# A new instruction plan for a fused recurrence and gated unit: transfers in plan order, three x buffers, gates multiplied in place

## The chip, the cores and the metric

One core of one Trainium2 chip runs the kernel. The time is the device time of the core in microseconds; the median of eight runs is compared. Five engines run side by side, each through its own list of instructions, in order: PE (matrix products and transposes), DVE (vector), ACT (activation functions), POOL (GpSimd) and SP (here it only issues loads). Results of PE stand in PSUM, eight banks of 512 fp32 columns; everything else stands in SBUF.

## What is computed

Inputs are x and two gates of 4 x 6336 x 256, a vector of 256 and three small weights. The first half is a gated linear recurrence over time, the second a gated unit with a causal convolution of five taps:

```python
a_t = np.exp(c * sig_r * np.log(np.clip(a_base, 1e-06, 1.0 - 1e-06))[None, None, :])   # c = 8, sig_r = sigmoid(r_gate)
norm = np.sqrt(np.maximum(1.0 - a_t * a_t, 1e-06))
x_gated = norm * sig_i * x
for t in range(S):
    h = a_t[:, t] * h + x_gated[:, t]
    y[:, t] = h
...
gate_pre = sum(conv_w[k] * y[t - (K - 1 - k)] for k in range(K))
out = (sigmoid(gate_pre) * (y @ w_val)) @ w_out
```

78.4 MB are read and 26 MB written.

## The kernel before

The 25,344 time steps of all four sequences are cut into 27 chunks: 512, then 23 of 1024, then 512, 512 and 256. A chunk's loads lay time over partitions; the recurrence needs channels on partitions, so PE transposes between the two. For a chunk `c` these steps run (`h` is the half of 128 channels, `s` the sub-chunk of 512 steps):

- loads on SP's queue: `ldri.c` (both gates, 1 MB each for a full chunk) and `ldx.c` (x, 1 MB), L216 to L224;
- ACT: `tanh.c` over both gates (L290), in place; a sigmoid is half of (tanh + 1);
- PE and ACT: `srT.c.h` transposes the r gate (L295), `exp.c.h` writes a_t (L304);
- POOL: `e.c.h` squares a_t (L310), `s1.c` adds 1 to the i gate (L318), `u.c` multiplies it with x (L345) into `uring`. After `u.c` the slot of the i gate and the slot of x are free for later loads;
- ACT: `sq` takes the root for one to three chunks at once (L354). Its table differs from that of tanh and exp, so each `sq` has two table loads around it (L472);
- PE, DVE: `nT.c.s` transposes the root (L367), `xg.c.s` multiplies it into `uring` (L374), `xgT.c.h` transposes back (L382), `scan.c.h` runs the recurrence (L395) into `yring`;
- PE, ACT, DVE: `conv.c.s` (L407) and `tg.c.s` (tanh, L417, into `tgr`), `val.c.s` (L425) and `gv.c.s` (L430, the product, into `gvr`), `out.c.s` (L439) with `gvr` as the stationary operand;
- `osbD` on DVE (L454) or `osbA` on ACT (L450) copies the result to SBUF, and `store.c.s` sends it out on ACT's queue (L459).

For chunks 0 and 1 (`X_PE`) the x of `u` is brought to PSUM by PE (`xc`, L327) and multiplied on DVE (`ux`, L335) instead of on POOL. `wc` converts the weights on ACT (L282, L284).

The order of all of this is written out in `PLAN`, a list of words such as `tanh.5.-1` (operation, chunk, half or sub-chunk, PSUM bank or -1), found beforehand by a search. `tc.manual_schedule()` keeps it, so each engine's list is the plan's words of that engine in the plan's order. Buffers are rings: three slots for each gate (`NRI`), two for x (`NX`), four for `uring` (`NU`), two each for `tgr` and `gvr`, five for the output (`NOSB`).

Each transfer signals its landing on one of eight semaphores, which are handed out in turn; a transfer may be issued only once the transfer eight turns earlier has landed. A store waits for this on ACT, in ACT's list; what stands behind it there waits with it. In the built program the turns do not follow the plan throughout: from turn 49 to turn 111 most transfers stand one to three places off. The store of chunk 8's first half has turn 71, so it waits for turn 63, which is the load of x for chunk 14.

Of the kernel before, what the change touches and what calls it, by code (L numbers as in the profile page):

```python
# [16 lines left out]
X_PE = [0, 1]  # L17
NRI = 3
NX = 2
NA = 5  # L20
NE = 5
NU = 4
# [3 lines left out]
NGV = 2  # L26
# [7 lines left out]
ldri.0.-1 ldri.1.-1 ldx.0.-1 ldx.1.-1 ldri.2.-1 ldw.-1 tanh.0.-1 srT.0.0.7 srT.0.1.5 exp.0.1.-1 exp.0.0.-1 e.0.0.-1  # L34
tanh.1.-1 e.0.1.-1 xc.0.1.0 xc.0.0.6 ux.0.0.-1 xc.1.2.1 u.0.-1 sq.0.1.-1 ux.1.2.-1 srT.1.0.0 ldri.3.-1 xc.1.1.5
ldx.2.-1 nT.0.0.7 srT.1.1.4 exp.1.0.-1 xg.0.0.-1 ux.1.1.-1 exp.1.1.-1 xc.1.0.0 tanh.2.-1 xc.1.3.5 e.1.1.-1 ux.1.0.-1
e.1.0.-1 wc.-1 srT.2.0.3 s1.2.-1 srT.2.1.2 xgT.0.0.4 exp.2.0.-1 scan.0.0.-1 exp.2.1.-1 e.2.0.-1 u.1.-1 tanh.3.-1
ldx.3.-1 ldri.4.-1 e.2.1.-1 u.2.-1 srT.3.1.3 srT.3.0.6 xgT.0.1.1 sq.1.2.-1 s1.3.-1 ldx.4.-1 ldri.5.-1 nT.2.0.7
nT.2.1.0 u.3.-1 xg.2.0.-1 exp.3.1.-1 xg.2.1.-1 nT.1.1.7 scan.0.1.-1 nT.1.0.5 tanh.4.-1 xg.1.1.-1 conv.0.0.0 xg.1.0.-1
xgT.2.0.3 e.3.1.-1 ldx.5.-1 xgT.1.1.4 ldri.6.-1 xgT.1.0.2 scan.1.1.-1 tg.0.0.-1 exp.3.0.-1 s1.4.-1 srT.4.1.1  # L40
exp.4.1.-1 scan.1.0.-1 val.0.0.4 e.3.0.-1 tanh.5.-1 srT.4.0.6 gv.0.0.-1 conv.1.0.0 u.4.-1 scan.2.0.-1 xgT.2.1.7
tg.1.0.-1 srT.5.1.5 srT.5.0.4 exp.4.0.-1 scan.2.1.-1 val.1.0.0 exp.5.1.-1 e.4.1.-1 ldx.6.-1 ldri.7.-1 exp.5.0.-1
gv.1.0.-1 conv.2.0.6 tanh.6.-1 e.5.1.-1 out.0.0.4 conv.1.1.0 osbD.0.0.-1 e.4.0.-1 val.2.0.2 tg.1.1.-1 val.1.1.4
e.5.0.-1 store.0.0.-1 tg.2.0.-1 out.1.0.0 conv.2.1.6 osbD.1.0.-1 s1.5.-1 sq.3.3.-1 gv.1.1.-1 u.5.-1 gv.2.0.-1
out.2.0.0 out.1.1.4 osbD.2.0.-1 osbD.1.1.-1 s1.6.-1 nT.3.1.3 ldri.8.-1 nT.3.0.2 ldx.7.-1 val.2.1.0 tg.2.1.-1 xg.3.0.-1
xg.3.1.-1 store.1.0.-1 u.6.-1 tanh.7.-1 gv.2.1.-1 xgT.3.1.7 nT.4.0.6 scan.3.1.-1 srT.6.0.1 srT.6.1.4 xgT.3.0.2
nT.4.1.0 nT.5.1.5 exp.6.0.-1 xg.4.0.-1 s1.7.-1 ldri.9.-1 xg.4.1.-1 exp.6.1.-1 srT.7.0.1 xg.5.1.-1 ldx.8.-1 nT.5.0.6
scan.3.0.-1 exp.7.0.-1 out.2.1.4 e.6.1.-1 tanh.8.-1 xgT.4.1.3 srT.7.1.7 xg.5.0.-1 conv.3.0.0 e.7.0.-1 osbD.2.1.-1
scan.4.1.-1 conv.3.1.4 u.7.-1 store.1.1.-1 tg.3.0.-1 xgT.4.0.6 srT.8.0.2 tg.3.1.-1 scan.4.0.-1 srT.8.1.0 exp.7.1.-1
val.3.1.4 exp.8.1.-1 gv.3.1.-1 e.6.0.-1 conv.4.1.6 ldx.9.-1 exp.8.0.-1 ldri.10.-1 xgT.5.0.3 store.2.0.-1 tg.4.1.-1  # L50
out.3.1.4 e.7.1.-1 scan.5.0.-1 tanh.9.-1 xgT.5.1.7 val.3.0.0 e.8.0.-1 conv.4.0.2 gv.3.0.-1 osbD.3.1.-1 e.8.1.-1
tg.4.0.-1 scan.5.1.-1 val.4.1.4 s1.8.-1 val.4.0.0 sq.6.3.-1 out.3.0.2 gv.4.1.-1 u.8.-1 gv.4.0.-1 osbD.3.0.-1 out.4.0.0
out.4.1.2 osbD.4.0.-1 srT.9.1.6 osbD.4.1.-1 nT.8.1.5 s1.9.-1 ldri.11.-1 nT.6.1.4 xg.8.1.-1 exp.9.1.-1 conv.5.0.2
ldx.10.-1 xg.6.1.-1 store.3.0.-1 tanh.10.-1 e.9.1.-1 nT.6.0.4 nT.7.1.1 xg.6.0.-1 nT.7.0.0 xgT.6.1.5 xg.7.0.-1 u.9.-1
xgT.6.0.4 xg.7.1.-1 srT.9.0.6 scan.6.0.-1 nT.8.0.7 exp.9.0.-1 conv.5.1.0 tg.5.0.-1 scan.6.1.-1 tg.5.1.-1 xgT.7.1.2
s1.10.-1 ldri.12.-1 store.2.1.-1 tanh.11.-1 val.5.1.0 ldx.11.-1 xg.8.0.-1 srT.10.1.3 srT.10.0.6 gv.5.1.-1 e.9.0.-1
val.5.0.4 conv.6.1.0 gv.5.0.-1 exp.10.1.-1 u.10.-1 srT.11.1.7 scan.7.1.-1 store.3.1.-1 store.4.1.-1 conv.6.0.4
tg.6.1.-1 exp.10.0.-1 srT.11.0.1 xgT.7.0.0 tg.6.0.-1 val.6.0.2 scan.7.0.-1 exp.11.0.-1 e.10.0.-1 out.5.0.4 ldri.13.-1
store.4.0.-1 ldx.12.-1 exp.11.1.-1 osbD.5.0.-1 out.5.1.0 e.10.1.-1 tanh.12.-1 conv.7.0.6 osbD.5.1.-1 e.11.0.-1
val.6.1.4 gv.6.0.-1 gv.6.1.-1 out.6.0.2 tg.7.0.-1 e.11.1.-1 store.5.1.-1 osbD.6.0.-1 xgT.8.1.6 xgT.8.0.7 s1.11.-1  # L60
out.6.1.4 scan.8.1.-1 sq.9.3.-1 val.7.0.2 u.11.-1 gv.7.0.-1 osbD.6.1.-1 conv.7.1.2 scan.8.0.-1 srT.12.0.1 srT.12.1.6
nT.9.0.0 nT.9.1.4 s1.12.-1 ldri.14.-1 nT.11.0.5 xg.9.0.-1 exp.12.0.-1 nT.10.0.7 ldx.13.-1 xg.9.1.-1 store.6.1.-1
xg.11.0.-1 store.5.0.-1 tg.7.1.-1 xgT.9.1.0 e.12.0.-1 scan.9.1.-1 exp.12.1.-1 out.7.0.2 tanh.13.-1 val.7.1.4 u.12.-1
osbD.7.0.-1 conv.8.0.0 gv.7.1.-1 nT.10.1.2 xgT.9.0.3 xg.10.1.-1 tg.8.0.-1 srT.13.0.6 scan.9.0.-1 s1.13.-1 ldri.15.-1
store.7.0.-1 tanh.14.-1 val.8.0.0 ldx.14.-1 out.7.1.4 xg.10.0.-1 e.12.1.-1 conv.8.1.2 gv.8.0.-1 srT.13.1.7 osbD.7.1.-1
store.6.0.-1 tg.8.1.-1 u.13.-1 xgT.10.0.1 srT.14.0.0 scan.10.0.-1 exp.13.0.-1 srT.14.1.4 out.8.0.2 exp.14.0.-1
xgT.10.1.6 store.7.1.-1 osbD.8.0.-1 exp.13.1.-1 conv.9.0.0 e.14.0.-1 exp.14.1.-1 scan.10.1.-1 ldx.15.-1 val.8.1.2
ldri.16.-1 tg.9.0.-1 nT.11.1.7 val.9.0.4 e.13.0.-1 store.8.0.-1 tanh.15.-1 gv.8.1.-1 conv.9.1.0 gv.9.0.-1 e.14.1.-1
out.8.1.2 val.9.1.4 osbD.8.1.-1 tg.9.1.-1 e.13.1.-1 xg.11.1.-1 store.8.1.-1 gv.9.1.-1 xgT.11.0.3 out.9.0.0 s1.14.-1
sq.12.3.-1 scan.11.0.-1 out.9.1.6 xgT.11.1.5 u.14.-1 osbD.9.1.-1 osbD.9.0.-1 val.10.0.6 srT.15.1.4 scan.11.1.-1  # L70
conv.10.0.2 s1.15.-1 nT.12.1.1 ldri.17.-1 tg.10.0.-1 nT.12.0.0 xg.12.1.-1 ldx.16.-1 srT.15.0.5 exp.15.1.-1 xg.12.0.-1
conv.10.1.2 gv.10.0.-1 u.15.-1 exp.15.0.-1 xgT.12.0.0 val.10.1.6 scan.12.0.-1 tg.10.1.-1 nT.13.1.1 store.9.0.-1
tanh.16.-1 conv.11.0.4 gv.10.1.-1 nT.13.0.3 e.15.0.-1 ldri.18.-1 nT.14.0.0 xg.13.1.-1 out.10.1.6 ldx.17.-1 xg.14.0.-1
xg.13.0.-1 tg.11.0.-1 e.15.1.-1 srT.16.0.2 osbD.10.1.-1 out.10.0.0 tanh.17.-1 val.11.0.6 osbD.10.0.-1 s1.16.-1
xgT.12.1.3 gv.11.0.-1 srT.16.1.1 conv.11.1.4 u.16.-1 scan.12.1.-1 exp.16.1.-1 val.11.1.6 tg.11.1.-1 srT.17.1.0
exp.16.0.-1 gv.11.1.-1 xgT.13.0.5 srT.17.0.4 store.10.0.-1 exp.17.1.-1 conv.12.0.2 scan.13.0.-1 e.16.0.-1 ldri.19.-1
store.9.1.-1 exp.17.0.-1 nT.14.1.0 ldx.18.-1 xgT.13.1.7 tg.12.0.-1 xg.14.1.-1 e.17.1.-1 scan.13.1.-1 store.10.1.-1
tanh.18.-1 out.11.0.2 xgT.14.0.4 e.16.1.-1 conv.12.1.0 osbD.11.0.-1 val.12.1.6 scan.14.0.-1 e.17.0.-1 tg.12.1.-1
out.11.1.2 val.12.0.0 s1.17.-1 gv.12.1.-1 sq.15.3.-1 gv.12.0.-1 out.12.1.6 u.17.-1 osbD.11.1.-1 out.12.0.4
osbD.12.1.-1 xgT.14.1.2 val.13.0.0 osbD.12.0.-1 conv.13.0.6 scan.14.1.-1 s1.18.-1 srT.18.0.3 ldri.20.-1 srT.18.1.5  # L80
tg.13.0.-1 nT.16.1.4 ldx.19.-1 store.12.0.-1 exp.18.1.-1 nT.17.0.2 gv.13.0.-1 u.18.-1 conv.13.1.6 store.11.0.-1
store.11.1.-1 exp.18.0.-1 xg.16.1.-1 nT.15.1.5 xg.17.0.-1 nT.15.0.1 tg.13.1.-1 xg.15.1.-1 val.13.1.2 xg.15.0.-1
tanh.19.-1 out.13.0.4 gv.13.1.-1 e.18.1.-1 ldri.21.-1 xgT.15.0.1 osbD.13.0.-1 conv.14.0.6 ldx.20.-1 scan.15.0.-1
e.18.0.-1 store.12.1.-1 tg.14.0.-1 srT.19.0.5 nT.17.1.0 exp.19.0.-1 nT.16.0.7 s1.19.-1 val.14.0.2 xg.17.1.-1
tanh.20.-1 xg.16.0.-1 xgT.15.1.5 gv.14.0.-1 srT.19.1.1 u.19.-1 scan.15.1.-1 out.13.1.2 xgT.16.0.7 exp.19.1.-1
srT.20.1.0 osbD.13.1.-1 srT.20.0.6 exp.20.1.-1 conv.14.1.4 scan.16.0.-1 exp.20.0.-1 e.19.0.-1 out.14.0.2 ldx.21.-1
ldri.22.-1 tg.14.1.-1 val.14.1.0 osbD.14.0.-1 e.19.1.-1 tanh.21.-1 xgT.16.1.5 conv.15.0.6 gv.14.1.-1 conv.15.1.2
e.20.1.-1 scan.16.1.-1 xgT.17.0.4 tg.15.1.-1 e.20.0.-1 scan.17.0.-1 tg.15.0.-1 srT.21.0.5 val.15.0.0 s1.21.-1
out.14.1.2 gv.15.0.-1 sq.18.3.-1 val.15.1.6 osbD.14.1.-1 s1.20.-1 srT.21.1.4 out.15.0.0 gv.15.1.-1 osbD.15.0.-1
u.20.-1 xgT.17.1.7 conv.16.0.2 scan.17.1.-1 store.13.0.-1 nT.18.1.1 nT.18.0.0 nT.19.1.6 xg.18.1.-1 tg.16.0.-1  # L90
nT.20.1.7 xg.18.0.-1 u.21.-1 ldri.23.-1 store.13.1.-1 exp.21.1.-1 val.16.0.2 xg.19.1.-1 xg.20.1.-1 ldx.22.-1 nT.20.0.1
store.14.0.-1 exp.21.0.-1 gv.16.0.-1 nT.19.0.6 xgT.18.0.7 store.15.0.-1 tanh.22.-1 xg.20.0.-1 out.15.1.4 xg.19.0.-1
# [48 lines left out]
def kernel(  # L141
# [54 lines left out]
    with tc.manual_schedule():  # L196
# [19 lines left out]
        def op_ldri(k, bank):  # L216
            c = k[0]
            n = CHUNKS[c]
            for e, src in ((0, rf), (1, if_)):
                nc.sync.dma_start(gate[:, slot(c, e), 0:n * H].rearrange("p (j d) -> p j d", d=D), toks(src, c, 0, n))  # L220
# [286 lines left out]
```

## The time and profile before

| what | value |
|---|---|
| median of 8 runs | 310.05 us (309.07 to 311.32) |
| the profiled execution | 309.97 us, of which its span is 307.9 us |
| granted TensorE clock, mean | 0.97 |
| transfers | 104.74 MB, mean 340 GB/s |
| `scan` L395, chunks of 1024 | 46 of 2.336 us |
| `tanh` L290, chunks of 1024 | 23 of 3.625 us |
| `u` L345, chunks of 1024 | 22 of 4.123 us |
| `gv` L430 / `osbD` L454 | 49 of 1.210 us / 41 of 1.210 us |
| `tg` L417 / `osbA` L450 | 49 of 1.033 us / 8 of 1.010 us |
| table loads L472 | 22 of 1.283 us |

The span is the time from the first instruction to the last; the other 2.07 us lie around it. "Busy" is the time in which an engine works on an instruction; issuing a transfer is not counted. Instructions of one engine overlap a little where they follow each other closely, so counts times means come out some per cent above the busy time. Where a chain of waits is told, each engine's idle time is put down to what ended it.

### The profile page before, as it was taken

To read this page: it belongs to the slowest core of one execution; us is meant where nothing else is said; L and a number is where in the kernel's file an instruction comes from. 1 tells how busy PE (TensorE), PEld (TensorE's weight loads), DVE (VectorE), ACT (ScalarE), POOL (GpSimd) and SP (SyncE) were. 2 spreads that over 40 slices of the span, in tenths; PEclk is the share of its full clock that TensorE was granted. 3 is DMA by queue.
4 is the path that set the end of the run, shared out by engine and by line. 5 is a ranking of instruction groups with operands and counts; after the bars stand their busy time and mean duration, and the time that the engine had idled before them with its cause. 6 is when DMAs were issued, how large, how long until landed. Compare 5 with 4: busy or idle time off the path is not lost.

```text
span 307.9 us, 6305 instructions
## 1 busy us (share of the span) xinstructions
PE 244.2 (79%) x2597; PEld 166.3 (54%) x2627; DVE 252.3 (82%) x208; ACT 278.2 (90%) x185; POOL 235.3 (76%) x118
## 2 busy tenths in 40 slices
PE   0571587868878887799589998988899987999994
PEld 0231454457537564656266665665666655555763
DVE  1052189479898999999499999999999998989893
ACT  6899999999999999998699999999999989858632
POOL 3229999997998999899996899989959993039000
PEclk9997589999999999999989999999999999999999
DMA  7999999998995999999999997999898764182555
GB/s 291 425 376 424 387 422 374 396 368 331 363 415 204 417 409 426 422 424 422 424 427 383 350 400 274 376 425 426 327 362 317 268 250 143 63 339 108 204 212 235
DMA packets 19466, 104.74 MB, mean 340 GB/s; under 512 B 2151, under 2 KB 2670, under 8 KB 10606
## 3 DMA queue, kind: packets, MB, share of 16 engines
q1 hardware_dynamic: 12224, 78.39, 64.5%
q10 hardware_dynamic: 7214, 25.96, 21.1%
q8 instruction: 20, 0.33, 0.4%
q14 instruction: 8, 0.07, 0.1%
HBM read 78.39 MB, written 25.95 MB: 339 GB/s over the span
## 4 chain that ended last, share of the span: by engine, by line
PE 30%; DVE 23%; ACT 15%; DMA 14%; issue 12%; POOL 3%; ACTq 1%; SPq 1%; DVEq 0%
DVE yring L395 13%; PE pp L407 8%; PE pp L439 7%; DMA gate<-in_i_gate_dram 6%; DMA xr<-in_x_dram 5%; PE pp L425 5%; DVE gvr L430 5%; PE pp L367 4%; ACT tgr L417 4%; DVE osb L454 4%; ACT aring L304 4%; ACT gate L290 3%; POOL uring L345 3%; DMA out_dram<-osb 3%; DVE uring L374 2%
## 5 line engine op out<-in xcount | busy, mean ns | idle before, releaser
L310 POOL TENSOR_TENSOR ering<-aring 128x1024 f32<-128x1024 f32 (+2 forms) x54 | 93.7, 1757 | 35.7 <-ACT aring L304 34.1
L395 DVE TENSOR_TENSOR_SCAN yring<-aring,yring,pp 128x1024 bf16<-128x1024 f32 (+2 forms) x52 | 113.4, 2192 | 3.6 <-PE pp L382 3.4
L345 POOL TENSOR_TENSOR uring<-gate,xr 128x2048 bf16<-128x2048 bf16 (+2 forms) x25 | 96.1, 3848 | 4.0 <-PE pp L382 2.6
L290 ACT ACTIVATE gate<-gate 128x4096 bf16<-128x4096 f32 (+2 forms) x27 | 90.2, 3340 | 6.7 <-DMA xr<-in_x_dram 3.8
L407 PE MATMUL pp<-yring,diag 64*64 64x512 bf16 (+13 forms) x1224 | 64.9, 339 | 5.5 <-DVE yring L395 2.3
L430 DVE SCALAR_TENSOR_TENSOR gvr<-tgr,pp 128x1024 bf16<-128x1024 bf16 (+1 forms) x50 | 59.4, 1200 | 8.9 <-ACT tgr L417 6.4
L439 PE MATMUL pp<-wo,gvr 128*128 128x256 bf16 x396 | 52.7, 279 | 13.7 <-DVE gvr L430 8.0
L304 ACT ACTIVATE aring<-pp,khf 128x1024 f32<-128x1024 bf16 (+2 forms) x54 | 59.3, 1144 | 3.8 <-PE pp L295 2.0
L417 ACT ACTIVATE tgr<-pp 128x1024 bf16<-128x1024 f32 (+1 forms) x50 | 50.5, 1024 | 10.0 <-PE pp L407 8.6
L439 PEld LDWEIGHTS <-gvr 128*128 128x128 bf16 x396 | 42.5, 115 | 23.5 <-DVE gvr L430 11.1
L425 PE MATMUL pp<-yring,wv 128*128 128x512 bf16 (+1 forms) x170 | 47.7, 376 | 7.8 <-DVE osb L454 2.2
L454 DVE COPY osb<-pp 128x1024 f32<-128x1024 f32 x41 | 49.0, 1210 | 5.9 <-PE pp L439 5.8
L318 POOL TENSOR_SCALAR gate<-gate 128x2048 bf16<-128x2048 bf16 (+2 forms) x25 | 44.5, 1783 | 5.4 <-ACT gate L290 5.4
L407 PEld LDWEIGHTS <-diag 64*64 64x64 bf16 x1224 | 30.3, 107 | 30.5 <-issue 14.2
L354 ACT ACTIVATE ering<-ering,b 128x4096 bf16<-128x4096 f32 (+4 forms) x16 | 46.5, 2933 | 0.1
L374 DVE TENSOR_TENSOR uring<-uring,pp 128x1024 bf16<-128x1024 bf16 (+1 forms) x50 | 32.0, 671 | 13.9 <-PE pp L367 13.6
L295 PE MATMUL pp<-ident_b,gate 128*128 128x128 bf16 x396 | 30.3, 225 | 14.5 <-ACT gate L290 11.9
L295 PEld LDWEIGHTS <-gate 128*128 128x128 bf16 x396 | 25.7, 100 | 22.9 <-ACT gate L290 14.6
L367 PE MATMUL pp<-ident_f,ering 128*128 128x128 f32 x198 | 32.3, 303 | 5.2 <-ACT ering L354 3.9
L382 PE MATMUL pp<-ident_f,uring 128*128 128x128 f32 x198 | 31.3, 280 | 5.9 <-ACT tgr L417 3.5
L367 PEld LDWEIGHTS pp<-ident_f,ering 128*128 128x128 f32 x198 | 27.8, 208 | 11.4 <-ACT ering L354 4.8
L425 PEld LDWEIGHTS <-wv 128*128 128x128 bf16 x200 | 18.8, 98 | 23.8 <-issue 11.0
(33 smaller groups left out, 86.2 us busy)
## 6 DMA issues: line engine op xcount, KB each, us to landing
out_dram<-osb ACTq DMA_DIRECT2D x49, 512.0 KB, 7.5
gate<-in_r_gate_dram SPq DMA_DIRECT2D x23, 1024.0 KB, 11.6
gate<-in_i_gate_dram SPq DMA_DIRECT2D x23, 1024.0 KB, 9.5
xr<-in_x_dram SPq DMA_DIRECT2D x23, 1024.0 KB, 9.9
gate<-in_r_gate_dram SPq DMA_DIRECT2D x3, 512.0 KB, 8.3
gate<-in_i_gate_dram SPq DMA_DIRECT2D x3, 512.0 KB, 10.6
xr<-in_x_dram SPq DMA_DIRECT2D x3, 512.0 KB, 3.4
yring<-in_moe_w_val_dram SPq DMA_DIRECT2D x1, 256.0 KB
```

Source lines behind the costliest of these rows:

```text
L290: nc.scalar.activation(out=tgate[:, s0:s0 + 2, 0:w], in_=gate[:, s0:s0 + 2, 0:w], func=ACT.Tanh, scale=0.5)
L304: nc.scalar.activation(out=dst, in_=src, func=ACT.Exp, scale=khf[:, h:h + 1], bias=khf[:, h:h + 1])
L310: nc.gpsimd.tensor_tensor(out=ering[:, c % NE, h * n:(h + 1) * n], in0=a, in1=a, op=ALU.mult)
L345: nc.gpsimd.tensor_tensor(out=u, in0=t, in1=xt, op=ALU.mult)
L367: nc.tensor.transpose(out=pp[:, d0:d0 + P], in_=src[:, w, :], identity=ident_f[:])
L395: nc.vector.tensor_tensor_scan(out=yring[:, h, y0:y0 + n], data0=aring[:, c % NA, h, 0:n], data1=src, initial=prev, op0=ALU.mult, op1=ALU.add)
L407: nc.tensor.matmul(out=pp[col * HP:(col + 1) * HP, b0 + d0:b0 + d1], lhsT=diag[r * HP:(r + 1) * HP, h, kk, :], rhs=yring[r * HP:(r + 1) * ...
L417: nc.scalar.activation(out=tgr[:, nth[k] % NTG, :, 0:n], in_=two(live["conv", k], n), func=ACT.Tanh, scale=0.5)
L425: nc.tensor.matmul(out=pp[:, (bank + m) * BANK:(bank + m) * BANK + n], lhsT=wv[:, hk, m, :], rhs=yring[:, hk, y0:y0 + n], start=(hk == 0), ...
L430: nc.vector.scalar_tensor_tensor(out=gvr[:, nth[k] % NGV, :, 0:n], in0=tgr[:, nth[k] % NTG, :, 0:n], scalar=1.0, in1=two(live["val", k], n ...
L439: nc.tensor.matmul(out=pp[:, bank * BANK + j * D:bank * BANK + (j + 1) * D], lhsT=gvr[:, nth[k] % NGV, m, 0:n].rearrange("c (p q) -> c q p ...
L454: nc.vector.tensor_copy(out=dst, in_=src)
```

## The change

The plan is replaced by another of 896 words (before 876). The steps are the same but for these differences.

- Every transfer goes through `dma`, which ties it to the transfer before it in the program, so that the eight semaphores are handed out in the plan's order. The store of chunk 8's first half now has turn 69 and waits for turn 61, a store (chunk 6's first half).
- The gates are loaded by two words, `ldr` and `ldi`, so that other transfers can stand between them. Chunk 0's `tanh` is cut into `tanh` (r gate) and `tanhi` (i gate).
- `X_PE` is empty: `xc` and `ux` are gone, and chunks 0 and 1 have `s1` and `u` on POOL like the others.
- `wc` moves from ACT to POOL.
- `NX` is 3 instead of 2, `NU` 3 instead of 4. `gvr` is gone: `gv` writes into `tgr`, and `out` reads `tgr`.
- 13 outputs are copied by ACT (`osbA`) and 37 by DVE (`osbD`); before they were 9 and 41. The groups of `sq` are the same.
- In the set-up the logarithm of the sigmoid is Ln(1 + e) straight from the exponential, clipped after it, without three small DVE steps; the first table load is put between the two small loads; small constants share the last slot of `osb`.
- POOL's instructions are kept in order one by one (`keep`) instead of by the schedule.

```diff
-X_PE = [0, 1]
+X_PE = []
-NX = 2
+NX = 3
-NU = 4
+NU = 3
-NGV = 2
...
+        def dma(queue, dst, src):
+            i = queue.dma_start(dst, src)
+            if turn:
+                tc.add_manual_dep(i.ins, turn[-1].ins.name,
+                                  mybir.DependencyInfo(mybir.DependencyClass.NoSync, mybir.DependencyReason.DATA),
+                                  reason="turn of the transfers")
+            turn.append(i)
...
-        nc.scalar.activation(out=kln[:], in_=ksig[:], func=ACT.Ln)
+        nc.scalar.activation(out=kln[:], in_=kex[:], func=ACT.Ln, bias=1.0)
...
-                nc.scalar.copy(out=wv[:, hk, :, :].rearrange("p m (i c) -> p i m c", i=2),
-                               in_=wvf[:, hk, :].rearrange("p (i m c) -> p i m c", i=2, m=2))
-            nc.scalar.activation(out=wo2[:], in_=wof, func=ACT.Copy, scale=0.5)
+                keep(nc.gpsimd.tensor_scalar(out=wv[:, hk, :, :].rearrange("p m (i c) -> p i m c", i=2),
+                                             in0=wvf[:, hk, :].rearrange("p (i m c) -> p i m c", i=2, m=2),
+                                             scalar1=1.0, scalar2=1.0, op0=ALU.mult, op1=ALU.mult))
+            keep(nc.gpsimd.tensor_scalar(out=wo2[:], in0=wof, scalar1=0.5, scalar2=1.0, op0=ALU.mult, op1=ALU.mult))
...
-            s0 = slot(c, 0)
-            nc.scalar.activation(out=tgate[:, s0:s0 + 2, 0:w], in_=gate[:, s0:s0 + 2, 0:w], func=ACT.Tanh, scale=0.5)
+            s0, s1 = slot(c, 0), slot(c, 0) + (1 if c == 0 else 2)
+            nc.scalar.activation(out=tgate[:, s0:s1, 0:w], in_=gate[:, s0:s1, 0:w], func=ACT.Tanh, scale=0.5)
...
-            nc.vector.scalar_tensor_tensor(out=gvr[:, nth[k] % NGV, :, 0:n], in0=tgr[:, nth[k] % NTG, :, 0:n], scalar=1.0,
+            nc.vector.scalar_tensor_tensor(out=tgr[:, nth[k] % NTG, :, 0:n], in0=tgr[:, nth[k] % NTG, :, 0:n], scalar=1.0,
...
-                                     lhsT=gvr[:, nth[k] % NGV, m, 0:n].rearrange("c (p q) -> c q p", q=q)[:, j, :],
+                                     lhsT=tgr[:, nth[k] % NTG, m, 0:n].rearrange("c (p q) -> c q p", q=q)[:, j, :],
```

The beginning of the new plan, up to the first group of two roots (`sq.1.2`), ACT's words in order: `tanh.0 exp.0.0 exp.0.1 tanhi.0 sq.0.1 tanh.1 exp.1.0 exp.1.1 tanh.2 tg.0.0 exp.2.1 exp.2.0 tanh.3 sq.1.2`. Before they were `tanh.0 exp.0.1 exp.0.0 tanh.1 sq.0.1 exp.1.0 exp.1.1 tanh.2 wc exp.2.0 exp.2.1 tanh.3 sq.1.2`. POOL's words up to the same point are now `e.0.0 e.0.1 s1.0 u.0 wc s1.1 e.1.0 e.1.1 u.1 e.2.1 e.2.0`; before they were `e.0.0 e.0.1 e.1.1 e.1.0 s1.2 e.2.0 e.2.1`.

The loads begin in the order r0, i0, r1, x0, i1, weights, i2, r2, x1, i3, r3; before it was r0, i0, r1, i1, x0, x1, r2, i2, weights, r3, i3. The last loads are x25, i25, r25 behind those of chunk 26; before the last was x26.

## The prediction

> **What bounds the kernel now.** I read the page's shares first, then the windows by stage, then ACT's waits with a timeline, then SP's waits.
>
> ```profile
> span 307.9 us, 6305 instructions
> ...
> PE 244.2 (79%) x2597; PEld 166.3 (54%) x2627; DVE 252.3 (82%) x208; ACT 278.2 (90%) x185; POOL 235.3 (76%) x118
> ```
>
> ```profile
> core 0: us, PE busy (x) PEld busy (x) DVE busy (x) ACT busy (x) POOL busy (x), PEclk, DMA share, GB/s
> 0.00:37.50 37.50, 16.02 (x85) 9.76 (x86) 7.02 (x16) 32.65 (x23) 20.73 (x18) 0.85 0.96 378
> 37.50:110.00 72.50, 58.34 (x657) 40.42 (x666) 62.71 (x50) 71.95 (x43) 69.07 (x31) 0.98 0.93 368
> 110.00:170.00 60.00, 49.47 (x509) 34.04 (x503) 54.22 (x43) 55.76 (x35) 55.61 (x26) 0.97 1.01 417
> 170.00:190.00 20.00, 17.46 (x197) 11.70 (x201) 19.87 (x15) 19.97 (x11) 18.42 (x9) 1.00 0.92 359
> 190.00:250.00 60.00, 52.99 (x594) 37.57 (x595) 59.50 (x47) 59.69 (x40) 54.78 (x27) 1.00 0.91 349
> 246.00:304.00 58.00, 52.42 (x608) 34.76 (x608) 52.94 (x44) 41.63 (x38) 20.65 (x14) 1.00 0.50 192
> ```
>
> ACT sets the pace from 37.5 to 250: it idles 0.55, 4.24, 0.03 and 0.31 us in those four stretches. From 170 to 250 DVE is as full (79.37 of 80). Behind 246 ACT has room (41.63 of 58) and DVE and PE, both near 52.5, share the end. So a gain on ACT counts until 246, behind it only PE or DVE work counts.
>
> Of ACT's 4.24 us between 110 and 170, 3.82 are one hole:
>
> ```profile
> 143.67 1.07 ACT L417 ACTIVATE tgr<-pp 128x1024 bf16<-128x1024 f32 x1
> 148.10 0.34 ACTq L459 DMA_DIRECT2D out_dram<-osb  x1
> 148.56 3.62 ACT L290 ACTIVATE gate<-gate 128x4096 bf16<-128x4096 f32 x1 [3.82 <-DMA xr<-in_x_dram]
> ```
>
> ```profile
> 135.30 0.40 SPq L224 DMA_DIRECT2D xr<-in_x_dram  x1
> ```
>
> The tanh of chunk 15 did not wait for its own data: that L290 reads no x. Ahead of it in ACT's list stands the store of chunk 8's first half (148.10), whose turn waits for the load of x for chunk 14, issued at 135.30. It left when that x had landed, and ACT stood for it.
>
> SP's waits show what the loads hang on:
>
> ```profile
> SPq L220 <- POOL uring L345: 88.7, 12, 13.7
> SPq L224 <- POOL uring L345: 74.7, 9, 18.4
> ```
>
> Gate and x loads leave when a `u` frees a slot. POOL is 91 to 95% busy from 37.5 to 250, so a late `u` is a late load and, three chunks on, a late tanh.
>
> **Start.** Before:
>
> ```profile
> 5.68 1.91 ACT L290 ACTIVATE gate<-gate 128x2048 bf16<-128x2048 f32 x1 [0.48 <-DMA gate<-in_i_gate_dram]
> ...
> 10.64 3.62 ACT L290 ACTIVATE gate<-gate 128x4096 bf16<-128x4096 f32 x1 [0.47 <-DMA gate<-in_i_gate_dram]
> ...
> 20.75 3.60 ACT L290 ACTIVATE gate<-gate 128x4096 bf16<-128x4096 f32 x1
> 24.25 0.70 ACT L282 CAST wv<-yring 128x256 bf16<-128x256 f32 x2
> 24.85 0.63 ACT L284 ACTIVATE wo<-yring 128x512 bf16<-128x512 f32 x1
> ...
> 32.49 3.71 ACT L354 ACTIVATE ering<-ering,b 128x4096 bf16<-128x4096 f32 x1
> 36.22 1.28 ACT L472 ACT_TABLE_LOAD   x1
> ```
>
> Before, the table load behind the first pair of roots ends at 37.50; call this mark A. After, by ACT's words in order: without ksig's steps ACT's 0.64 us wait goes and the exp table is in at 4.6 (before 5.20). tanh of r alone takes 1.05 (the 128x1024 row): 5.65. The transposes cost the gap seen before the first exp, 1.13: 6.8. Two exp 1.45, tanhi 1.05, table 1.28, root 1.15, table 1.28: 13.0. i1 is the fifth load; the fifth before (x0) had landed by 11.88, where PE's wait for it ends. tanh 3.61, gap 1.13, two exp 2.3, tanh 3.6, `tg` 1.03, two exp 2.3, tanh 3.6: 30.6; the second gap, for the transposes of chunk 2, is covered by `tg`. Table 1.28, roots 3.71, table 1.28: 36.9. That is 0.6 early, and the first `tg` is done, which stood behind A before. POOL keeps up: `e` of chunk 0 done near 9.6, s1 1.05, u 2.16, the weights some 2.0 (between 1.3, twice the 0.354 of POOL's 128x64 row and once the 0.62 of its bf16 128x512 row, and 3.1, three times the 1.043 of its fp32 128x512 row), s1.1 behind tanh.1 at 18.5, two e to 22.8, u.1 4.12 to 26.9, two e to 30.7: the roots start at 31.9. If weights or x land 1.2 us late this cover is gone and A moves one for one. **Term: -0.6, between -2.5 and +1.5.**
>
> **From A to the group root of chunks 21 and 22** (before at 245.99, between its table loads). ACT's words in this stretch: the same 20 full tanh, 7 roots, 42 full exp; one exp of 512 less (-0.77), one osbA more (+1.01); the first `tg` done before A is made up by one more inside. **Term: +0.2.**
>
> The 3.82 hole: with turns in the plan's order the store of chunk 8 waits for a store eight turns back. The closest pair of a store behind a load in the new plan is chunk 12's second store behind i19, with 7.9 us of ACT work between by the rows' means; before, four pairs had 2.2, 2.4, 5.7 and 6.9, and one of the four opened the hole. DVE could have held ACT back later anyway: up to the root it has 200.4 us by counts where it had 203.0, and its idle 5.8 between 110 and 170 holds 3.6 us between 150 and 170, right behind the hole. **Term: -3.8, bounds -3.8 and 0; I take -3.8.**
>
> **Tail, from that root to the end** (61.9 us before). By the plan PE has one conv (1.21), one val (0.87) and one xgT (0.65, all as the chain of waits has them) less and one short srT (0.3) more: -2.5. DVE has one scan (2.34) and three osbD (3.63) less: -6.0. ACT has three osbA (3.03) and a short exp (0.77) more, one tg less: +2.8, into its 16 idle us. PE is then the fullest, 49.9 against DVE's 47.0, so the tail loses what PE loses. If DVE alone set it, 6.0; if ACT's hand-offs, 0. **Term: -2.5, between -6.0 and +2.8.**
>
> **What fewer buffers add.** `gvr` gone: a tanh of the convolution must wait until `out` two parts back has read `tgr`, where `gv` was enough. By the two plans, places with no ACT work between producer and waiting `tg` go from 8 of 48 (for gv) to 14 (for out). The 8 cost 1.3 us of ACT waiting on DVE L430; by that row the 14 cost 2.3, so +1.0. Behind a waiting tg stand exp, tanh and the stores. Bounds 0 and 14 x 0.9 (one out) = 12.6. `NU` 3: u must wait for xgT three chunks back, not four; places with no POOL work between go from 3 to 11. POOL's wait on PE L382 was 2.6 in 2; by that row 9.5 us on POOL, inside its 14.6 us of idle between 37.5 and 250, so 0 on ACT. Behind a waiting u stand s1, e and the loads it frees. Bounds 0 and 9.5. `NX` 3 takes the third slot from that store: x loads no longer wait for the u before last (74.7 us of SP waiting, hidden); 0, between -1.3 (ACT's idle time in the four stretches but for the hole) and 0. POOL's added 11 us (s1 and u of chunks 0 and 1, 1.05 + 1.90 + 2.16 + 4.12, weights) stand before A, costed there; DVE loses 4.1 of ux and PE 8.3 of xc there, into idle time. The same 84 loads, among them three of weights, and 50 stores are issued, at 0.33 to 0.5 us each as before; cutting `ldri` in two lets r leave without i, and costs nothing on SP, which mostly waits. **Term: +1.0.**
>
> **Two rules against it.** The Trainium skill, Perfetto Trace Analysis, section Identifying the Most-Contended Engine, calls the engine of highest occupancy the bottleneck. That is ACT at 90%, and the new plan gives it 2.9 us more (four osbA, less wc): by the page alone 312.9. The windows say that the added work lies where ACT idles. DMA: Bandwidth & Descriptors, section Where 436 GB/s comes from, lets HBM bind at some 358 GB/s (though it lists 425 for a 16 MB transfer); at 358, 104.74 MB would need 293 us and no order of transfers could help. The window 110 to 170 moved 417 GB/s for 60 us, so the measurement decides against that floor.
>
> **Sum.** -0.6 + 0.2 - 3.8 - 2.5 + 1.0 = -5.7. The profiled execution took 309.97 (span 307.9 and 2.07 around it; the median of the runs is 310.05). 309.97 - 5.7 = **304.3**.
>
> **Rivals.** *(1) Slower: the ring u, i load, tanh.* SP's waits speak for it: each i leaves when a u ends, and u now hangs on xgT, which hangs on a full DVE. Against it: from 37.5 to 250 ACT waited once for a gate load, 0.42 us at 45.75. Price: if the 9.5 us of POOL's waits pass to ACT in full, 304.3 + 9.5 = 313.8. It makes the kernel slower once 6.6 of the 9.5 pass, a third of a microsecond for each of the 20 full tanh in the stretch. Chance 0.25. *(2) No change: ACT's idle time stays as it is.* Then A gives 0.6, the hole 3.8, and ACT's 2.9 us are added, with +1.0: -0.5, 309.5. For it: ACT at 90%; against it: 16 idle us behind 246. Chance 0.12. *(3) DVE sets the end.* Its work falls by 4.8 (osbD), 4.1 (ux) and 0.5 (ksig), 9.4 in all, of which the part before A is idle time: tail -6.0 in place of -2.5, no coupling: 299.8. For it: DVE at 99% from 170; against it: PE next. Chance 0.13. *(4) It does not do what it says:* the hole opens at another store, 304.3 + 3.8 = 308.1; inside the forecast's own range, 301 to 308.2. Forecast, with this, 0.50.
>
> **How the numbers follow.** 0.3%, 0.93 us, is about what a measurement of this kernel can tell from no change. Faster: 0.50 + 0.13 + a quarter of (2) 0.03 = 0.66. Same: the rest of (2) less a little, 0.08. Slower: (1) and that little, 0.26. Range 299.5 to 314: rival 3 to rival 1 at its price; about 0.17 is left out, most of it above, where the 12.6 of `tgr` would come on top.
>
> **What would show it.** A table load behind the first pair of roots ending near 36.9; no ACT gap above 2 us between 37.5 and 245; that later root starting near 241.8; ACT's tail waits on PE, not DVE. Wrong if ACT waits for gate loads by many small gaps, if POOL's waits for the transposes of xgT pass 10 us, or if DVE idles over 5 us between 170 and 240.

## The result and the profile after

| kernel | median | ratio to before, 95% interval | span of the profiled execution |
|---|---|---|---|
| before | 310.07 us (32 runs) | 1 | 307.9 us |
| changed | 312.87 us (11 runs, 312.0 to 317.61) | 1.0105 [1.008, 1.013] | 312.4 us |

The change makes the kernel about 1% slower; forecast was 304.3 us. Medians count every run; the ratios leave out runs more than 1.5% above the fastest of the same kernel, here the one of 317.61. The profiled execution of the changed kernel took 314.16 us, 1.3 above its median, so what its profile shows as lost is too large by about as much. The page of the changed kernel (span, busy times, and the granted clock of PE in 40 slices):

```profile
span 312.4 us, 6288 instructions
...
PE 249.4 (80%) x2586; PEld 169.7 (54%) x2615; DVE 245.0 (78%) x196; ACT 281.9 (90%) x187; POOL 245.9 (79%) x125
...
PEclk9999997998797999999999999999999999999999
```

DVE's work fell by 7.3 us and ACT's rose by 3.7, the way the plan's words said (9.4 and 2.9 in the prediction). PE's did not fall: it lost `xc` and yet is busy 5.2 us longer. The windows by stage, columns as in the prediction:

```profile
0.00:37.50 37.50, 15.28 (x91) 10.01 (x93) 6.83 (x11) 33.07 (x23) 30.00 (x24) 1.00 0.97 392
37.50:110.00 72.50, 57.24 (x531) 39.44 (x536) 53.77 (x42) 66.02 (x38) 62.59 (x28) 0.91 0.90 348
110.00:170.00 60.00, 51.50 (x565) 34.21 (x571) 56.18 (x43) 56.99 (x34) 54.65 (x26) 1.00 0.98 386
170.00:190.00 20.00, 18.31 (x218) 12.68 (x218) 19.58 (x17) 19.97 (x15) 18.49 (x9) 1.00 0.92 356
190.00:250.00 60.00, 52.53 (x564) 36.72 (x570) 56.77 (x45) 57.01 (x35) 54.06 (x26) 1.00 0.90 355
```

From 37.5 to 110 us ACT idles 6.48 us where it idled 0.55, from 190 to 250 it idles 2.99 where it idled 0.31, and PE's clock from 37.5 to 110 reads 0.91 where it read 0.98. Three marks cut the time as the prediction did: A (end of the table load behind the first pair of roots), the start of the root of chunks 21 and 22, and the end of the span.

| us | before | predicted | changed | before, turns tied (below) |
|---|---|---|---|---|
| start to A | 37.50 | 36.9 | 36.94 | 37.21 |
| A to root | 208.49 | 205.9 | 217.68 | 205.94 |
| root to end | 61.9 | 59.4 | 57.8 | 61.9 |

All of the loss lies between A and the root. ACT's timeline there, with the table load that ends at A, five of its waits and the root at the end (start, length, what it computes, then the idle time before it and what ended that):

```profile
35.66 1.28 ACT L491 ACT_TABLE_LOAD   x1
...
42.92 1.21 ACT L324 ACTIVATE aring<-pp,khf 128x1024 f32<-128x1024 bf16 x1 [2.35 <-PE pp L315]
...
52.23 2.11 ACT L437 ACTIVATE tgr<-pp 128x1024 bf16<-128x1024 f32 x2 [1.07 <-PE pp L427]
...
82.91 1.02 ACT L437 ACTIVATE tgr<-pp 128x1024 bf16<-128x1024 f32 x1 [0.91 <-PE pp L427]
...
145.19 3.62 ACT L305 ACTIVATE gate<-gate 128x4096 bf16<-128x4096 f32 x1 [2.49 <-DMA gate<-in_i_gate_dram]
...
215.52 3.62 ACT L305 ACTIVATE gate<-gate 128x4096 bf16<-128x4096 f32 x1 [1.11 <-DMA gate<-in_r_gate_dram]
...
254.62 3.71 ACT L374 ACTIVATE ering<-ering,b 128x4096 bf16<-128x4096 f32 x1
```

The stall in front of a store is gone. In its place stand some dozen waits, none above 2.5 us: 3.9 us in all for `srT` (L315) and 3.1 for `conv` (L427) on PE, 3.6 for gate loads, and one of 1.16 that is put down to POOL. From A to the root ACT's idle time adds up to 12.5 us, against 5.1 in before and 2.5 with tied turns.

### The profile page after: what moved, and what is told of

The parts are those of the page before. It is cut to its first block, busy times and chain, and to the rows that moved or that the text cites. A ratio compares the mean times of both kernels' runs of the same rounds, so it can differ in the third digit from the quotient of the medians.

```text
span 312.4 us, 6288 instructions
## 1 busy us (share of the span) xinstructions
PE 249.4 (80%) x2586; PEld 169.7 (54%) x2615; DVE 245.0 (78%) x196; ACT 281.9 (90%) x187; POOL 245.9 (79%) x125
## 4 chain that ended last, share of the span: by engine, by line
ACT 29%; PE 28%; DVE 12%; DMA 11%; issue 10%; POOL 7%; ACTq 1%; SPq 0%; DVEq 0%; POOLq 0%
ACT ering L374 8%; PE pp L427 8%; ACT tgr L437 6%; ACT aring L324 6%; POOL uring L365 5%; PE pp L445 5%; PE pp L459 5%; PE pp L387 5%; DVE yring L415 4%; DMA gate<-in_r_gate_dram 4%; ACT gate L305 4%; DVE tgr L450 4%; DMA xr<-in_x_dram 4%; DMA gate<-in_i_gate_dram 3%; ACT L491 3%
## 5 line engine op out<-in xcount | busy, mean ns | idle before, releaser
L365 POOL TENSOR_TENSOR uring<-gate,xr 128x2048 bf16<-128x2048 bf16 (+2 forms) x27 | 102.3, 3790 | 13.1 <-PE pp L402 5.6
L450 DVE SCALAR_TENSOR_TENSOR tgr<-tgr,pp 128x1024 bf16<-128x1024 bf16 (+1 forms) x50 | 59.5, 1202 | 25.7 <-PE pp L445 20.7
L427 PE MATMUL pp<-yring,diag 64*64 64x512 bf16 (+13 forms) x1224 | 68.5, 353 | 2.5 <-DVE yring L415 0.8
L459 PE MATMUL pp<-wo,tgr 128*128 128x256 bf16 x396 | 53.0, 280 | 9.3 <-DVE tgr L450 5.9
L459 PEld LDWEIGHTS <-tgr 128*128 128x128 bf16 x396 | 42.0, 115 | 21.0 <-DVE tgr L450 10.0
L474 DVE COPY osb<-pp 128x1024 f32<-128x1024 f32 x37 | 44.5, 1214 | 8.6 <-PE pp L459 7.9
L338 POOL TENSOR_SCALAR gate<-gate 128x2048 bf16<-128x2048 bf16 (+2 forms) x27 | 47.5, 1759 | 3.3 <-ACT gate L305 3.3
L427 PEld LDWEIGHTS <-diag 64*64 64x64 bf16 x1224 | 31.7, 111 | 29.6 <-issue 15.1
L315 PE MATMUL pp<-ident_b,gate 128*128 128x128 bf16 x396 | 33.3, 237 | 16.1 <-ACT gate L305 10.1
L387 PE MATMUL pp<-ident_f,ering 128*128 128x128 f32 x198 | 34.1, 315 | 12.9 <-ACT ering L374 8.8
L315 PEld LDWEIGHTS <-gate 128*128 128x128 bf16 x396 | 28.4, 108 | 25.4 <-ACT gate L305 15.0
```

Of the source, the lines that this page charges most:

```text
L365: keep(nc.gpsimd.tensor_tensor(out=u, in0=t, in1=xt, op=ALU.mult))
L387: nc.tensor.transpose(out=pp[:, d0:d0 + P], in_=src[:, w, :], identity=ident_f[:])
L427: nc.tensor.matmul(out=pp[col * HP:(col + 1) * HP, b0 + d0:b0 + d1], lhsT=diag[r * HP:(r + 1) * HP, h, kk, :], rhs=yring[r * HP:(r + 1) * ...
L450: nc.vector.scalar_tensor_tensor(out=tgr[:, nth[k] % NTG, :, 0:n], in0=tgr[:, nth[k] % NTG, :, 0:n], scalar=1.0, in1=two(live["val", k], n ...
L459: nc.tensor.matmul(out=pp[:, bank * BANK + j * D:bank * BANK + (j + 1) * D], lhsT=tgr[:, nth[k] % NTG, m, 0:n].rearrange("c (p q) -> c q p ...
```

## Experiments

**The tie alone.** In the kernel before, `dma()` ties each transfer to the one before it, as in the change; plan and buffers stay.

```diff
-            nc.sync.dma_start(xr[:, c % NX, ...], toks(xf, c, 0, CHUNKS[c]))
+            dma(nc.sync, xr[:, c % NX, ...], toks(xf, c, 0, CHUNKS[c]))
```

> The kernel before, its plan and buffers unchanged, with only the turns of the transfers tied to the plan's order. Theory A (the stall was its own loss): the 3.82 us stall of ACT in front of the store of chunk 8 goes and nothing takes its place, so 306.2 to 307.5 us. Theory B (slack elsewhere eats it): DVE, at 99% behind 170 us, or another store's turn holds ACT by as much, so 309.5 to 310.5 us with no ACT gap above 2 us at 144 to 149 but more small ones behind it.

306.88 us, ratio 0.9892 [0.9866, 0.9918]. ACT's timeline where the stall was:

```profile
145.21 0.34 ACTq L221 DMA_DIRECT2D out_dram<-osb  x1
145.65 3.62 ACT L302 ACTIVATE gate<-gate 128x4096 bf16<-128x4096 f32 x1 [1.23 <-DMA gate<-in_i_gate_dram]
```

The store no longer holds ACT; the tanh of chunk 15 still waits 1.23 us, for its own i. So the hole was worth 2.6 us of its 3.8 in this stretch (table above), and 3 us of the time, as in theory A, but for the wait of 1.23 us in its place. The opposite edit, the changed kernel without the tie:

> The changed kernel without the tie between transfers, so that the turns on the eight semaphores are again handed out as the program is built. If ties matter in the new plan as they did in the plan before (3.0 us), 314 to 317 us with a stall of ACT in front of a store; if the plan leaves room around its stores at any order, 312.5 to 313.5 us.

313.65 us, 1.0116 [1.0083, 1.0149]: no difference from the changed kernel that can be told. The tie gains 1% in the old plan and nothing that can be told in the new one.

**Fewer buffers.** First the old plan in the new buffers:

> The plan before with tied turns in the buffers of the changed kernel: three x slots, three uring slots, gates multiplied in place in tgr. Theory 'buffers' (the fewer buffers cost the 7 us that were lost between the first pair of roots and the root of chunks 21 and 22): 5 to 8 us above the run with tied turns alone. Theory 'word order' (the new order of words itself meets PE and the gate loads too late): at most 2 us above that run.

341.58 us. This run prices nothing: the old plan has 20 halves where `u` stands ahead of the transposes of the chunk three back and 15 places where `tg` stands ahead of `out` two parts back, so in these buffers those values are overwritten before they are read, and other waits arise. It shows that the old order cannot be had with three `uring` slots. The next two took the room from the output slots and have the same fault in small: two sub-chunks are copied out before the store that still needs their slot, which therefore sends another's result.

> The changed kernel with a separate buffer for the product again (gvr, two slots), paid for with one output slot (four instead of five). Theory 'buffers': the waits of tgr for PE's out (4.0 us in 2) go, and with them up to 5 us of the small gaps: 308 to 310 us. Theory 'word order': 312 to 313.5 us, the waits for out become waits for gv.

> The changed kernel with four uring slots again, paid for with one output slot (four instead of five). Theory 'buffers, ring of u': POOL's wait for the transposes of xgT (5.6 us in 4) falls below 2 us, u and the i loads behind it come earlier, ACT's waits for gate loads (4.1 us) go: 308 to 310 us. Theory 'word order': 312 to 313.5 us, since u waits for what stands ahead of it in POOL's list all the same.

317.82 and 313.49 us, both without meaning for the buffers. Repeated with all five output slots, the room now won by reading the bf16 identity as the upper halves of the fp32 one:

```diff
-        ident_b = const.tile([P, P], BF16, name="ident_b")
-        nc.vector.tensor_copy(out=ident_b[:], in_=ident_f[:])
+        ident_b = ident_f[:].bitcast(BF16)[:, 1:2 * P:2]
```

> The changed kernel with its plan and its five output slots, and a separate buffer for the product again (gvr, two slots); the room for it comes from reading the bf16 identity as the high halves of the fp32 identity. Theory 'buffers': the two waits of tgr for PE's out in the tail (4.0 us) go and the time falls by 2 to 4 us, to 309 to 311 us. Theory 'word order': the waits for out turn into waits for gv or conv of nearly the same length, at most 1 us faster, 312 to 313 us.

> The changed kernel with its plan and its five output slots, and four uring slots again (room as in the run with gvr). Theory 'buffers, ring of u': POOL's waits for xgT (5.6 us in 4) fall below 2 us and the time falls by 2 to 5 us, to 308 to 311 us. Theory 'word order': u still stands behind the same words of POOL and its i loads behind it, so at most 1 us faster, 312 to 313 us.

314.05 us (1.0124 [1.0071, 1.0177]) and 312.69 us (1.0066 [1.0034, 1.0099]), against 1.0105 [1.008, 1.013] for the changed kernel. A separate buffer for the product brings nothing that can be told, a fourth `uring` slot some 0.4%, with intervals that overlap, although POOL's waits for `xgT` (5.6 us) are gone from its profile. As waits, these two buffers are not what cost the time; what they forced on the order of the words is another matter. `NX` was not tried by itself.

**Short loads.** From chunk 4 on each load brings 128 steps of its chunk (both kernels compute the rest from what the slot held):

```diff
-            n = CHUNKS[c]
+            n = CHUNKS[c] if c < 4 else P
```

> The changed kernel, but from chunk 4 on each gate and x load brings only the first 128 steps of its chunk (the rest of the chunk is computed from what the slot held before), so that a load lands a few us after its issue. Theory 'late loads' (u ends late, the i load behind it lands just when its tanh is due, and everything behind waits): ACT's small gaps between 37.5 and 250 us fall from 11.8 us to below 6, and the time falls by 5 us or more, to 308 us or less. Theory 'order of the engines' words': the gaps on PE's transposes and convolutions stay, only the 4 us of direct waits for loads go at most, 309 to 313 us.

> The kernel before with tied turns, with the same short loads from chunk 4 on (the rest of the chunk is computed from what the slot held before). Both theories: its loads had 1 to 8 us to spare, so at most 2 us faster than with full loads, 304.5 to 307 us. If it falls by as much as the changed kernel does, landing times are no part of the difference between the two plans.

309.94 us (0.9979 [0.9948, 1.0011]) and 303.73 us (0.9788 [0.9748, 0.9828]): both fall by about 3 us. ACT's idle time from A to the root falls in the changed kernel only to 9.0 us. So late loads alone do not make the difference, against the first theory; what stays are the waits for PE, 7.1 of the 9.0 us.

**PE's clock.** What PE does behind a pair or a triple of roots, sixteen fp32 transposes of `nT`, took this long in the changed kernel at two places:

```profile
35.69 3.69 PE L387 MATMUL pp<-ident_f,ering 128*128 128x128 f32 x16 [3.38 <-ACT ering L374]
...
169.56 2.20 PE L387 MATMUL pp<-ident_f,ering 128*128 128x128 f32 x16
```

The same work, 1.7 times as long. In the starts of PE's transposes two rates are seen: fp32 transposes of `nT` start 0.213 or 0.121 us apart, bf16 ones of `srT` 0.107 or 0.056. In the changed kernel PE runs at the slow rate at most places from 5 to 45 us and again around 70 and 97; in the kernel before it does so around 8, from 31 to 40 and, behind the hole, from 153 to 156, and with tied turns only around 8 and from 31 to 39. The test fills PE's idle time with transposes of the identity into free banks:

```diff
+        def op_hot(k, bank):
+            for j in range(k[0]):
+                nc.tensor.transpose(out=pp[:, bank * BANK + j % 4 * P:bank * BANK + (j % 4 + 1) * P],
+                                    in_=ident_f[:], identity=ident_f[:])
...
-srT.2.0.2
+hot.10.6 srT.2.0.2
```

> The changed kernel with filler on PE: 121 transposes of the identity into banks that are free, put in 13 places up to 97 us where PE stood idle for 1.1 to 4.5 us, and no other word moved. Theory 'cold PE' (a PE that idles is granted half the clock: at 5 to 45, 69 to 72, 79 to 82 and 95 to 100 us its fp32 transposes start 0.213 us apart instead of 0.121, and ACT's small gaps are waits for those): the transposes behind the first pair of roots run at 0.12 us, ACT's gaps between 37.5 and 110 fall from 6.3 to below 2.5 us, and the time falls by 4 us or more, to 309 us or less, at best to 303. Theory 'order of the words' (the gaps come from what stands ahead of what, at any clock): the added work on PE brings at most 1 us, or costs, 312 to 314 us.

> The same with only the six fillers ahead of the transposes behind the first pair of roots (up to 36 us). Theory 'cold PE': the 2.35 us gap at 42.9 us and the 1.07 us one behind it go, 308 to 310 us, and PE stays warm behind them or does not; the run with all fillers tells. Theory 'order of the words': 312 to 314 us.

> The same with only the seven fillers behind the first pair of roots (45 to 97 us). Theory 'cold PE': the gaps at 77 to 109 us (2.8 us) go, the one at 42.9 stays, 310 to 312 us. Theory 'order of the words': 312 to 314 us.

> The kernel before with tied turns, and 47 filler transposes on PE in the three places between 21 and 36 us where it idles and falls to half the clock. Theory 'cold PE': its cold stretch (31 to 39 us) holds nothing that ACT waits for, since chunk 3 was transposed ahead of the roots, so at most 1 us faster than without, 305.9 to 307 us. If the filler brings as much here as in the changed kernel, a cold PE is no part of the difference between the plans.

The plan holds 107 fillers in 13 places, 62 of them in the first six and 45 in the later seven (the expectation speaks of 121 in all). All of them: 309.00 us, 0.9963 [0.9933, 0.9994], 3.9 us below the changed kernel by the medians. The start alone 312.32 (1.0059 [1.003, 1.0088]), the later seven alone 312.94 (1.0121 [1.007, 1.0172]). The old plan with tied turns: 306.31, 0.9887 against 0.9892 without. So filler brings the new plan 1.4% and the old one nothing that can be told. That more work on PE makes the kernel faster can't come from the order of the words alone. What changed on PE, first in the changed kernel, then with the fillers:

```profile
41.82 1.91 PE L315 MATMUL pp<-ident_b,gate 128*128 128x128 bf16 x16
```

```profile
34.85 3.63 PE L387 MATMUL pp<-ident_f,ering 128*128 128x128 f32 x16 [3.08 <-ACT ering L374]
...
40.14 1.06 PE L315 MATMUL pp<-ident_b,gate 128*128 128x128 bf16 x16
```

The transposes behind the first pair of roots stayed slow, against the expectation; `srT` behind them is fast, and ACT's wait of 2.35 us at 42.92 is 1.07 at 40.79. With the later seven alone ACT's waits for `conv` from A to the root fall from 3.1 us to 0.3, but those for gate loads rise from 3.6 to 6.2 and the time stays. The gain is less than was expected at best, and the profile with more filler says why:

> The changed kernel with more filler: 17 places, among them the start, the wait at 72 us and the one at 144 us, and fillers sized at 0.109 us each (201 transposes in all). Theory 'cold PE': the cold stretches that were left with the smaller fillers (5 to 17, 35 to 38, 73 to 76 and 144 to 147 us) go and the time falls a further 1 to 2 us below the 309.0 of the run with small fillers, to 307 to 308.3. Theory 'loads are what is left': 308.5 to 309.5, with PE warm and ACT still waiting some 4 us for gate loads.

311.46 us, 1.0018 [0.9994, 1.0042]: by the ratios half a per cent slower than with fewer. ACT's timeline with these fillers, 203 by the plan (201 in the expectation):

```profile
71.79 3.62 ACT L305 ACTIVATE gate<-gate 128x4096 bf16<-128x4096 f32 x1 [3.58 <-DMA gate<-in_i_gate_dram]
...
143.94 3.62 ACT L305 ACTIVATE gate<-gate 128x4096 bf16<-128x4096 f32 x1 [2.99 <-DMA gate<-in_i_gate_dram]
```

Every wait for `srT` between A and 110 us has gone, and the tanh of chunks 7 and 14 wait for their i instead: with its waits for PE gone ACT only comes sooner to a load that is not there. Part of the loss is the filler itself: A comes at 37.9, 1.0 us later than in the changed kernel. Then both at once:

> The changed kernel with the first 121 fillers and with the short loads from chunk 4 on (only the first 128 steps of a chunk are loaded). If a cold PE (3.9 us) and late loads (2.9 us) are two separate costs they add up: 306 to 306.7 us. If they are one cost seen twice (PE goes cold while it waits for late loads): 308 to 309.5 us. What then stands above the 303.7 of the kernel before with tied turns and short loads is the order of the words by itself.

302.73 us, 0.9760 [0.9727, 0.9794], 10.1 us below the changed kernel, where fillers brought 3.9 and short loads 2.9: more than their sum, which neither expectation had. The windows of this run, from its slowest execution (304.98):

```profile
37.50:110.00 72.50, 60.29 (x633) 44.54 (x636) 58.23 (x47) 70.64 (x41) 68.48 (x31) 0.95 0.30 105
110.00:170.00 60.00, 55.01 (x604) 36.49 (x592) 57.91 (x45) 59.46 (x38) 55.95 (x25) 1.00 0.33 125
```

ACT idles 1.9 and 0.5 us, although PE is slow from 40 to 45 us in this execution too. They are two costs, and each hides part of the other. With fillers and short loads the new plan is as fast as the old one with short loads and tied turns (0.9788). The old plan with both was not run; with short loads its ACT idles only 1.0 us from A to the root, so little is left to gain there, but that nothing remains for the order of the words by itself is not shown.

**Can the loads be mended by their order?** Only the words of the loads are moved, with the 107 fillers (i6 goes ahead of r6, x7 ahead of r10, x11 ahead of i11 and i12, r15 behind i14, and so on). It is less than the expectation says: x4 still stands behind i6, x7 behind i9 and x10 behind i12.

> The changed kernel with the first 121 fillers, and with the words of the loads alone put in another order: loads that stood behind a load whose slot came free later go ahead of it (x4 no longer behind i6, x7 behind i9, x10 and x11 behind i12, and each r behind the i that is due sooner); every byte is loaded and every other word stays. Theory 'late loads and a cold PE together' (short loads brought 6.3 us on top of the fillers): ACT's waits for gate loads (4.3 us with the fillers alone) fall below 2 us and the time lies 2 to 4 us below the 309.0 with fillers alone, 305 to 307. If the loads are late because of the u they wait for and not because of their order on the queue: 308.5 to 309.5.

308.94 us, 0.9962 [0.9937, 0.9987], no gain. In its profiled execution A comes 3 us later than with the fillers alone, since loads of the start were moved too, and ACT waits 6.3 us for i, 2.8 of them before A; from A to the root it is 3.5, where it was 3.4. So the order on the queue is not shown to be the cause, and not excluded, the less so as the x loads that the expectation names stay behind the same i loads but for x11.

**A plan with room.** The same words in the same buffers, in an order from a search over a model that was fitted to these traces and counts PE at half clock in four stretches and landings up to 2.6 us late; all engines' words may move.

> The changed kernel with its words put in another order by a search of my own, over a model of the four engines and the transfers that counts PE at half its clock in four stretches and landings up to 2.6 us late; same words, same buffers, same ties, no filler. If slack against a cold PE and late loads is what the changed plan lacked, 303 to 307 us, below both kernels; if the model misses the cause, 310 us or more.

> The same order with 62 filler transposes in six places up to 65 us. If the order already leaves room for a cold PE, within 1 us of the run without filler; if not, 2 to 4 us below it.

305.46 us, 0.9855 [0.9813, 0.9896], and with fillers 306.70, 0.9891 [0.985, 0.9932]. Without filler it is the fastest kernel here that does the whole work, 4.9 us below before in the same session, and 1.4 us below the old plan with tied turns by the medians, with intervals that overlap. In its PE list `srT` of chunk 3 stands ahead of the last `nT` of chunk 2, and ACT has no wait above 0.2 us from A to 97 us, although PE runs at its slow rate at most places up to 38 us there too. The fillers add nothing here: 1.2 us more by the medians, with intervals that overlap. What this order mended is the PE side: from A to the root ACT's waits for `srT` and `conv` fall from 7.0 us to 2.5, while those for i gates are 3.9. Each i is still issued only 9.5 us ahead of its tanh on average, as in the changed kernel (9.6). The page's clock row (what such a row is worth is said at the end):

```profile
PEclk9999999999999799999999989999999999999999
```

## Why the prediction was wrong

- **Start, -0.6.** A at 36.94, predicted 36.9, in part by luck: the table load behind the first root ends at 12.26 us, 0.7 ahead of the 13.0 of the sum, and the transposes of chunk 2, "covered by `tg`" there, make ACT wait 1.07 us.
- **The hole, -3.8.** The mechanism was right (the tie closes it, alone 3 us), the size 2.6 in this stretch: the tanh behind the store had a wait for i of 1.2 beneath it.
- **Work from A to the root, +0.2.** Right by count: ACT has the same instructions there but for one short exp less and one osbA more, and they add up to 213.7 us against 214.5 in before and 214.9 with tied turns. Behind a wait they overlap less, so that ACT's busy time there is 205.1 us against 203.4 in both.
- **Tail, -2.5.** Measured -4.1, inside its bounds; the waits of ACT in it are for PE, as said, but for one of 0.5 us for a gate load. It is no echo of the middle's loss, since it stays when that goes (57.1 us with fillers and short loads, 57.4 replanned). Why it is 1.6 us shorter than PE's count says stays open.
- **The step that failed is the term of +1.0, "what fewer buffers add"**, as the only one for new waits. In the profiled executions the stretch from A to the root is 11.7 us longer than with the old plan and tied turns, and 10.0 of them are idle time of ACT (12.5 against 2.5). The term priced the buffers (in place +1.0, `NU` 0, `NX` 0), which the runs put at nothing that can be told for the first and some 0.4% for the second, and took the rest of ACT's gap-free list over from the old plan. Two things were left out. PE's lost `xc` and its idle waits were booked as "into idle time", without asking whether PE would stay at its fast rate; fillers in these waits bring 1.4%. (That the lost `xc` itself made PE slow was not tested by putting it back. The clock column of the windows, 0.85 in the start of before, stood in the prediction's own fence and was not read, but it is no sure guide: it reads 1.00 in the start of the changed kernel.) And the distance from the issue of an i load to its tanh was looked at only by waits that ACT had before (0.42 us once), not in the new plan. From the trace, chunks 4 to 23, on average: `u` ends 17.0 us after its tanh starts in before, 23.0 in the changed kernel; so i, which leaves with that `u`, is issued 13.7 us ahead of its own tanh in before and 9.6 in the changed kernel, while its landing takes 9.5 us in the median there and 7.9 here.
- **Rival 1 (slower, 313.8)** named the ring `u`, i load, tanh, and the time came within 1 us of it. But its price was taken from the wait on `uring`, and without that wait the time stays (312.69); `u` still ends 22.2 us after its tanh then. That its place behind the squares in POOL's list makes it late is argued from the plan, not tested. The ring is one of the two costs: with more filler the loads take over (311.46), with both away 10.1 us go.
- **Rivals 2 and 3** fall with the sign: ACT's idle time did not stay, and DVE did not set the end (245.0 us of work in 312.4). Rival 4: no store holds ACT for long.
- **The figure by ACT's share alone, 312.9,** meets the median by luck. ACT's busy time did rise, by 3.7 us, but the loss lies in its waits: 7.4 us more idle time from A to the root than in before, while the tail is 4.1 us shorter. The other rule of the prediction, 293 us at 358 GB/s, would not have excluded the forecast in any case, since 293 lies below 304.3.
- **What would show it:** the root start at 241.8 (by the prediction's own terms, with the +1.0, it is 242.8) came at 254.6, and gaps of 2.35 and 2.49 us stand where none above 2 was to be. Of the three signs of error, the waits for gate loads appeared (4.1 us), POOL's waits for xgT (5.6 us, not 10) and DVE's idle time did not; PE's clock was not on the list.

Whether the wait at 42.92 us would go by moving `srT` of chunk 3 alone was not tried.

## What to carry to other kernels

An engine that is full by its share is so because every other one hands its work over in time; when the order changes, measure that spare time again, from each producer to its consumer and from each load's issue to its use, and don't carry the old idle time over. Two limits at the same height hide each other: take both away in one run before judging either. Read PE's rate, from the starts of its instructions, beside its busy time: here added work on an idle PE made the kernel faster by 1.4%.

## What the runs showed of the hardware

- PE has two rates, a factor of 1.8 to 1.9 apart, and is found at the slow one after idle waits: with fillers in them, the slow stretches at 23, 40 to 45, 69 and 97 us are gone, and new ones at 72.6 and 144 us stand behind waits for loads. The Trainium skill, TensorE: Matmul & The Clock Gate, section What's actually happening, tells of a clock gate that halves the clock after an idle window of some 3.4 us and frees it after a busy one. The two rates agree with a halving (0.107 and 0.056 us). The length does not quite: the slow stretch at 69 us in the changed kernel followed idle waits of 1.38 and 1.41 us only.
- The same idle wait has two outcomes: with tied turns PE idles 2.44 us from 60.9 and stays fast; with short loads it idles as long from 60.1, and is slow from 63.3 to 66.9. The section says that the window runs freely, which would fit; no run here shows where a window begins. The clock records show single slow stretches of 3.4 us, the page's length (69.0 to 72.4 in the changed kernel, 63.3 to 66.7 with short loads).
- The clock in the records can be wrong: in the changed kernel's profile it reads 1.00 from 25 to 40 us, where the sixteen transposes took 3.69 us. The durations decide. The page warns of this (section Seeing it yourself).
- The changed kernel's runs spread over 4.1 us (312.0 to 316.1, but for one of 317.6), those of before over 2.4. That an order at the limit of two waits spreads more is not shown: the six runs of the replanned kernel lie as far apart (304.5 to 308.5).
